# V rows requested over three pairs with the beacon rows last, and sums moved from the tail into the loop

## Chip, cores, metric

The kernel runs on one core of a Trainium2 chip. The metric is the time of one execution on the device in microseconds (us), lower is better. The profile's span, from the first to the last instruction, is some 2 us shorter than that time. Inside the text, moments are us from the start of the span. Executions of this kernel scatter by 1 to 2%, so small differences are read from the profiles' stages as well as from the times.

## The reference

Causal attention with 16 extra "beacon" keys and values per head, then a soft mixture of experts with 32 slots over all 4608 tokens. Cut to what matters:

```python
B, H, S, Nb, D = 8, 8, 576, 16, 64          # attention; E=8 experts, 4 slots each, F=1024
k_all = np.concatenate([beacon_k, k], axis=2)
v_all = np.concatenate([beacon_v, v], axis=2)
scores = q @ k_all^T / 8, causal over k, beacons always visible
x = softmax(scores) @ v_all                 # -> (B*S, H*D) = (4608, 512)
logits = x @ phi                            # (4608, 32)
d = softmax(logits, axis=0);  slot_input = d.T @ x
slot_out[e] = relu(slot_input[e] @ w1[e]) @ w2[e]
c = softmax(logits, axis=1);  out = c @ slot_out
```

## The kernel before

The loop runs over 32 pairs of heads, n = 0 to 31, four pairs to a batch (b = n // 4, g = n % 4). The order of instructions on each engine is the order of the program. Each pair has four score steps on TensorE, an exponential after each on ScalarE, causal masks on GpSimd, the attention matmuls of the pair before, normalisation and copies on VectorE. GpSimd also requests V and the experts' weights, because both are cast from f32 to f16 on the way in. SyncE requests q and k, five pairs ahead.

```python
    def score(n, st):                       # cut: tiles and offsets
        for (c, kn, u0, un, col) in steps[st]:
            for a in range(2):
                nc.tensor.matmul(sc[0:kn, a, col:col + un], kT..., qT..., start=True, stop=True)
        nc.scalar.activation(e, sc[:, :, 0:w], AF.Exp, scale=scale)
        for m, o in diag[st]:
            nc.gpsimd.affine_select(out=e[0:m, :, o:o + m], ...)          # causal mask

    def load_v(b, qd):                      # one quarter of a batch's V rows (cut: batches 0 and 1)
        nc.gpsimd.dma_start(out=vbuf[b % 2][32 * qd:32 * qd + 32, :], in_=...)

    def load_bv(b):                         # beacon rows: inside the first quarter's rows
        nc.gpsimd.dma_start(out=vbuf[b % 2][0:4 * H:4, 0:Nb * D], in_=beacon_v[b]...)

    # ahead of the loop
    for qd in range(4): load_v(0, qd)
    for i in range(3):  load_tail(0, i)
    for qd in range(4): load_v(1, qd)

    for n in range(NP):
        score(n, 0); transp(m, 0); score(n, 1)       # transp: q, k of a later pair, on TensorE
        turn_v(...)                                  # V quarters transposed on VectorE
        attend_head(n - 1, 0); xt_piece(n - 2)
        score(n, 2); transp(m, 1); load_more(m); score(n, 3)
        attend_head(n - 1, 1); normalize(n - 1)
        if n >= 6 and g == 3:      dt_piece(b - 1)
        if n >= 5 and g in (1, 2): logit_piece(b - 1, g - 1)
        if n >= 8 and g == 0:      add_si(si_products(b - 2))
        if n >= 5:
            x, y = divmod(n - 5, 4)
            if x + 3 < B and y < 2:
                load_v(x + 3, 2 * y); load_v(x + 3, 2 * y + 1)
            if y == 1 and x + 3 < B:
                load_bv(x + 3)
        # then some weights (load_w), on a schedule by n
    # tail: last pair, sums of batch 6, last logits, fold_si, dt_piece(L), col_sums(0, 4), si_half,
    # first_layer / turn_hidden / second_layer over four groups of two experts
    # (col_sums(4, 9) in the second group), scaling, output
```

The softmax here doesn't subtract the row's maximum and nothing guards it: scores larger than these inputs give would overflow.

Of the kernel before, what the change touches and what calls it, by code (L numbers as in the profile page):

```python
# [8 lines left out]
FP = mybir.dt.float32  # L9
# [8 lines left out]
def kernel(  # L18
# [13 lines left out]
    P = 128  # L32
# [125 lines left out]
    def turn_tail(b4, hf):  # L158
        turn(vt[b4].bitcast(FP).rearrange("p r e -> p e r")[0:96], vlast[0:96], hf)
# [52 lines left out]
    for qd in range(4):  # L212
        load_v(1, qd)
# [11 lines left out]
    eLh = const.tile([P, Nb + N], F16, name="eLh")  # L225
# [70 lines left out]
    def attend_head(n, a, dst=None):  # L296
        b, g = divmod(n, H // 2)
        dst = av[:, a, :] if dst is None else dst
        for i in range(NCH):
            m = P if i < 4 else UL  # L300
            for c in range(i + 1):
                kn = P if c < 4 else UL
                o, w = blk[(c, i)]
                nc.tensor.matmul(  # L304
                    dst[0:m, i * DD:(i + 1) * DD],
                    ex[n][0:kn, o + a * w:o + a * w + m],
                    vchunk(b, 2 * g + a, c, kn),
                    start=(c == 0), stop=(c == i))
# [48 lines left out]
    def dt_piece(b):  # L357
        dT[b] = sml.tile([P, NCH, NSL], F16, name="dT", tag="dT")
        tp = ps_tr.tile([P, NCH, NSL], F16, name="tr", tag="tr")
        for i in range(NCH):  # L360
            m = P if i < 4 else UL
            nc.tensor.transpose(tp[0:m, i, :], eLh[0:NSL, b * S + P * i:b * S + P * i + m],
                                idh[0:NSL, 0:NSL])
        nc.vector.tensor_copy(out=dT[b][:, 0:4, :], in_=tp[:, 0:4, :])
        nc.vector.tensor_copy(out=dT[b][0:UL, 4, :], in_=tp[0:UL, 4, :])
        nc.vector.memset(dT[b][0:Nb, 0, :], 0.0)
# [26 lines left out]
    def fold_si():  # L393
        tp = ps_tr.tile([P, NDC, NSL], FP, name="tr", tag="tr")
        for c in range(NDC):
            x = siacc[:, 256 * (c // 2):256 * (c // 2) + 256].rearrange("p (f r) -> p f r", r=2)
            nc.tensor.matmul(tp[:, c, :], x[:, :, c % 2], fold[:, :], start=True, stop=True)
        nc.vector.tensor_copy(out=siT[:, :, :], in_=tp[:, :, :])

    def load_more(m):  # L400
        if m + 5 < NP:
            load_pair(m + 5)

# [10 lines left out]
    for n in range(NP):  # L414
# [3 lines left out]
        if 5 <= n and m < NP:  # L418
            transp(m, 0)
        score(n, 1)  # L420
        if n < 5:
            transp(m, 0)
# [4 lines left out]
        if 13 <= n < 17:  # L427
            turn_tail(1, n - 13)
        if 2 <= n < 5:
            attend_head(n - 2, 0)  # L430
        elif n >= 5:
            attend_head(n - 1, 0)
# [6 lines left out]
        if m < NP:  # L439
            transp(m, 1)  # L440
            if n > 0:
                load_more(m)
        score(n, 3)
        if n == 0:
            hold(3)
            load_pair(3)
            nc.sync.dma_start(out=bkf[:, 1:B, :], in_=bks[:, 1:B, :])
            load_pair(4)
            load_more(0)
            load_more(1)  # L450
            nc.sync.dma_start(out=phif[:, :, :], in_=moe_phi.rearrange("(c p) e -> p c e", p=P))
        if n == 1:
            turn_v(0, 2)
            turn_v(0, 3)
            for y in range(4):
                turn_tail(0, y)
# [13 lines left out]
        if n >= 6 and g == 3:  # L470
            dt_piece(b - 1)
# [25 lines left out]
        if n >= 5:  # L497
            x, y = divmod(n - 5, 4)
            if x + 3 < B and y < 2:
                load_v(x + 3, 2 * y)  # L500
                load_v(x + 3, 2 * y + 1)
            if y == 1 and x + 3 < B:
                load_bv(x + 3)
        if 8 <= n < 11:
            load_tail(1, n - 8)
        want = n - 1 if n < 4 else n if n < 6 else 5 + 18 * (n - 5) // 25 if n < 24 else (
            18 + 9 * (n - 23) // 5)
        while wl < min(want, NPC) and not (n < 24 and n % 4 == 2):
            load_w(wl)
            wl += 1  # L510
# [3 lines left out]
    G = 4  # L514
    NG = N // (P * G)
    csp = scs[1][:, 0, :]
    rc = const.tile([P, NG * G], FP, name="rc")

    def etok(cg, j):
        o = Nb + cg * P * G  # L520
        return eLh[:, o:o + P * G].rearrange("p (t j) -> p t j", j=G)[:, :, j]

    def col_sums(c0, c1):
        for i in range(c0 * G, c1 * G):
            nc.tensor.matmul(csp[:, i:i + 1], etok(i // G, i % G)[0:NSL], ones[0:NSL, :],
                             start=True, stop=True)
# [7 lines left out]

    xt_piece(NP - 2)
    avl = [av[:, 0, :], scs[1][:, 1, :]]
    for a in range(2):
        attend_head(NP - 1, a, avl[a])
        normalize_head(NP - 1, a, avl[a])
    sp = si_products(L - 1)  # L540
    lps = [scs[0][:, hf, 0:S // 2] for hf in range(2)]
# [9 lines left out]
    last_logits(range(NDC - 1))  # L551
    xt_piece(NP - 1)
    add_si(sp)
# [4 lines left out]
    fold_si()  # L558
    dt_piece(L)
    col_sums(0, 4)  # L560
# [51 lines left out]
    for p in range(EP + 2):  # L612
# [4 lines left out]
        if p == 1:  # L617
            col_sums(4, NG)
            col_sum_factors()
# [58 lines left out]
```

## Time and profile before

| | before |
|---|---|
| time, median of the first 3 runs | 203.93 us (202.47 to 205.74) |
| span of the profiled run | 201.6 us, mean TensorE clock 0.90 |
| pair 6 starts / pair 31 starts | 39.0 / 150.5 |
| second layer ends / span ends | 173.3 / 201.6 |
| last packet of the loads ends | 169.7 |

The profiled run took 203.51 us.

### The profile page before, as it was taken

What the parts mean: (1) busy time and instruction counts of PE and PEld (TensorE: products, weight loads), DVE (VectorE), ACT (ScalarE), POOL (GpSimd) and SP (SyncE); (2) the same over time, 40 slices, a digit from 0 to 9 for tenths busy, and PEclk for the clock granted to TensorE, in tenths of its full rate; (3) what the DMA queues carried; (4) which work ended last, traced back from release to release, by engine and by line L of the source; (5) the groups of instructions that cost most, each with busy time, mean ns of one, the idle gap of its engine ahead of it and who ended that gap; (6) DMA issues with size and microseconds to landing.
All of it is one profiled execution on the core that took longest, in us unless ns stands there. A gap on an engine that the chain in (4) does not pass through costs nothing.

```text
span 201.6 us, 7189 instructions
## 1 busy us (share of the span) xinstructions
PE 161.2 (80%) x3056; PEld 106.9 (53%) x3056; DVE 137.3 (68%) x286; ACT 129.3 (64%) x189; POOL 110.7 (55%) x285
## 2 busy tenths in 40 slices
PE   6656977895699779969999999999997899788000
PEld 2434756663476547746777766667666654332000
DVE  4446677787188949995989988989855542599100
ACT  2783964786179837964898988898896122399000
POOL 8459689561668586856797577778768000000000
PEclk9975799999589988996999999999999969999855
DMA  6999989999999999999889999999999994099994
GB/s 185 265 267 329 330 217 204 256 252 262 290 265 281 247 203 227 283 265 186 258 174 289 253 294 261 284 222 211 217 214 211 215 211 83 22 400 418 419 423 197
DMA packets 20464, 50.84 MB, mean 252 GB/s; under 512 B 5456, under 2 KB 5456, under 8 KB 19408
## 3 DMA queue, kind: packets, MB, share of 16 engines
q0 software_dynamic: 8048, 21.74, 56.0%
q1 hardware_dynamic: 12240, 28.35, 39.0%
q8 instruction: 24, 0.39, 0.7%
q10 hardware_dynamic: 144, 0.29, 0.5%
q14 instruction: 8, 0.07, 0.1%
HBM read 62.65 MB, written 9.44 MB: 358 GB/s over the span
## 4 chain that ended last, share of the span: by engine, by line
PE 46%; DMA 20%; POOL 10%; DVE 10%; issue 4%; ACT 3%; DVEq 0%; POOLq 0%; ACTq 0%
DMA vbuf<-in_v_dram 20%; PE av L304 14%; PE sc L283 11%; PE tr L266 7%; POOL ex L292 5%; DVE arena L641 4%; PE tr L339 3%; DVE xb L315 2%; ACT ex L290 2%; PE tr L385 2%; PE av L606 2%; PE av L592 1%; PE sc L592 1%; POOL vbuf L162 1%; PE tr L350 1%
## 5 line engine op out<-in xcount | busy, mean ns | idle before, releaser
L290 ACT ACTIVATE ex<-sc 128x736 f16<-128x736 f32 (+1 forms) x124 | 102.0, 868 | 30.2 <-PE sc L283 29.6
L292 POOL TENSOR_SCALAR_AFFINE_SELECT ex<-ex 128x256 f16<-128x256 f16 (+1 forms) x155 | 57.3, 404 | 26.4 <-ACT ex L290 26.1
L304 PE MATMUL av<-vh,ex 128*128 128x65 f16 x854 | 40.6, 202 | 11.6 <-POOL ex L292 9.7
L304 PEld LDWEIGHTS <-ex 128*128 128x128 f16 x930 | 37.3, 109 | 23.7 <-issue 11.9
L283 PE MATMUL sc<-qT,kT 64*128 64x336 bf16 (+5 forms) x384 | 47.4, 300 | 2.9 <-ACT ex L290 1.6
L266 PE MATMUL tr<-idb,arena 64*64 64x64 bf16 x1152 | 32.3, 200 | 3.4 <-DMA arena<-in_k_dram 1.6
L266 PEld LDWEIGHTS <-arena 64*64 64x64 bf16 x1152 | 24.9, 113 | 13.9 <-issue 8.2
L272 DVE COPY qT<-tr 128x576 bf16<-128x576 bf16 x32 | 24.0, 751 | 6.4 <-PE tr L266 5.5
L315 DVE TENSOR_TENSOR xb<-av,r 128x640 f16<-128x640 f32 x31 | 25.6, 825 | 1.1
L283 PEld LDWEIGHTS <-kT 64*128 64x128 bf16 (+1 forms) x384 | 16.4, 100 | 17.1 <-issue 9.5
L272 DVE COPY kT<-tr 128x576 bf16<-128x576 bf16 x27 | 20.4, 755 | 5.9 <-PE tr L266 5.8
L151 DVE STREAM_TRANSPOSE vh<-vbuf 128x256 f32<-128x256 f32 x32 | 20.4, 655 | 2.0 <-DMA vbuf<-in_v_dram 1.4
L343 DVE COPY xT<-tr 128x592 f16<-128x592 f16 x32 | 13.9, 439 | 10.7 <-PE tr L339 10.7
L183 POOL DMA_DIRECT2D arena<-in_moe_w_dram x32 | 17.9, 564 | 0.2
L127 POOL DMA_DIRECT2D vbuf<-in_v_dram x27 | 15.1, 568 | 0.5 <-DVE xb L315 0.5
L339 PE MATMUL tr<-idh,xb 128*128 128x128 f16 (+1 forms) x160 | 14.0, 221 | 0.9 <-DVE xb L315 0.9
L639 ACT ACTIVATE arena<-fp,rc 128x512 f32<-128x512 f32 (+1 forms) x18 | 11.3, 673 | 5.4 <-PE fp L637 4.6
L314 DVE RECIPROCAL r<-av 128x10 f32<-128x10 f32 x31 | 6.9, 221 | 11.2 <-PE av L304 10.9
L641 DVE TENSOR_SCALAR arena<-fp,rc 128x512 f32<-128x512 f32 (+1 forms) x19 | 12.6, 731 | 0.4 <-PE fp L637 0.4
L637 PE MATMUL fp<-soh,eLh 128*128 128x512 f16 (+1 forms) x37 | 10.7, 371 | 2.4 <-ACT arena L639 1.6
L339 PEld LDWEIGHTS <-xb 128*128 128x128 f16 (+1 forms) x160 | 10.3, 102 | 1.2 <-DVE xb L315 1.0
L162 POOL DMA_DIRECT2D vbuf<-in_beacon_v_dram x7 | 3.8, 546 | 11.6 <-DMA vbuf<-in_v_dram 11.6
(98 smaller groups left out, 138.3 us busy)
## 6 DMA issues: line engine op xcount, KB each, us to landing
arena<-in_moe_w_dram POOLq DMA_DIRECT2D x32, 512.0 KB, 10.1
arena<-in_q_dram SPq DMA_DIRECT2D x32, 288.0 KB, 7.5
arena<-in_k_dram SPq DMA_DIRECT2D x31, 288.0 KB, 7.5
out_dram<-arena SPq DMA_DIRECT2D x8, 1024.0 KB, 9.5
vbuf<-in_v_dram POOLq DMA_DIRECT2D x30, 128.0 KB, 6.5
arena<-in_v_dram POOLq DMA_DIRECT2D x4, 128.0 KB, 7.7
out_dram<-arena SPq DMA_DIRECT2D x2, 256.0 KB, 2.7
out_dram<-arena SPq DMA_DIRECT2D x1, 512.0 KB, 3.2
```

Of the source, the lines that this page charges most:

```text
L127: nc.gpsimd.dma_start(out=vbuf[b % 2][32 * qd:32 * qd + 32, :], in_=bass.AP(tensor=v.tensor, offset=v.offset + lo, ap=[hs_, cs_, [1, TK * ...
L151: nc.vector.transpose(out=dst[:, e], in_=src.bitcast(FP).rearrange("p (j e) -> p e j", j=TK)[:, e])
L183: nc.gpsimd.dma_start(out=arena[:, wloc[m]:wloc[m] + WP], in_=src)
L266: nc.tensor.transpose(tp[po:po + 64, j, :], hi, idb[po:po + 64, po:po + 64])
L272: nc.vector.tensor_copy(out=dst, in_=src)
L283: nc.tensor.matmul(sc[0:kn, a, col:col + un], kT[n % 3][64 * a:64 * a + 64, P * c:P * c + kn], qT[n % 3][64 * a:64 * a + 64, u0:u0 + un], ...
L290: nc.scalar.activation(e, sc[:, :, 0:w], AF.Exp, scale=scale)
L292: nc.gpsimd.affine_select(out=e[0:m, :, o:o + m], in_=e[0:m, :, o:o + m], compare_op=AL.is_ge, fill=0.0, base=0, pattern=[[0, 2], [1, m]], ...
L304: nc.tensor.matmul(dst[0:m, i * DD:(i + 1) * DD], ex[n][0:kn, o + a * w:o + a * w + m], vchunk(b, 2 * g + a, c, kn), start=(c == 0), stop= ...
L315: nc.vector.tensor_tensor(out=xb[b % 2][:, :, 2 * g:2 * g + 2, :].rearrange("p i a d -> p a i d"), in0=avv[:, :, :, 0:D], in1=r5[:, :, :]. ...
L339: nc.tensor.transpose(tp[:, i, 0:m], xb[b % 2][0:m, i, 2 * g:2 * g + 2, :].rearrange("p h d -> p (h d)"), idh[0:m, 0:m])
L641: nc.vector.tensor_scalar(out=osb[:, j, c], in0=fp_[:, c], scalar1=rc[:, i:i + 1], scalar2=None, op0=AL.mult)
```

## The change

The intent: take the wait for V off GpSimd, where it holds up the masks; put the first masks ahead of V of batch 1; and shorten the tail. The diff, cut to its core:

```diff
-    for qd in range(4):
-        load_v(1, qd)                      # ahead of the loop
@@ in the loop
+        if n == 0:
+            load_v(1, 0)
         if n == 1:
+            for y in range(1, 4):
+                load_v(1, y)
+        if n == 2:
+            warm(4)                        # dummy matmuls ahead of the first attention
+            if n == 1:
+                warm(2)                    # ahead of transp(m, 1)
-        if n >= 5:
-            x, y = divmod(n - 5, 4)
-            if x + 3 < B and y < 2:
-                load_v(x + 3, 2 * y)
-                load_v(x + 3, 2 * y + 1)
-            if y == 1 and x + 3 < B:
-                load_bv(x + 3)
+        x, y = divmod(n - 4, 4)
+        if n >= 4 and x + 3 < B:
+            for qd in ((0,), (1, 2), (3,), ())[y]:
+                load_v(x + 3, qd)
+            if y == 2:
+                load_bv(x + 3)
-        want = n - 1 if n < 4 else n if n < 6 else 5 + 18 * (n - 5) // 25 if n < 24 else (...)
-        while wl < min(want, NPC) and not (n < 24 and n % 4 == 2):
+        want = n if n < 6 else n - (n - 2) // 4 if n < 24 else 18 + 9 * (n - 23) // 5
+        while wl < min(want, NPC):
@@ sums
+        if n == NP - 1:
+            dt_piece(b - 1)                # between score(n, 0) and score(n, 1)
         score(n, 1)
+        if n == NP - 1:
+            add_si(si_products(b - 1))
+            if n >= 8 and g == 0:
+                col_sums(b - 2, b - 1)     # ahead of attend_head(n - 1, 0)
@@ tail
+    for a in range(2):                     # last token chunk of the last pair first
+        attend_blocks(NP - 1, a, avl[a], [(c, 4) for c in range(NCH)])
     xt_piece(NP - 2)
-    sp = si_products(L - 1)
+    fold_si(0)                             # fold_si in halves, around xt_piece(NP - 1)
     xt_piece(NP - 1)
-    add_si(sp)
+    fold_si(1)
-    fold_si()
+    col_sums(6, 7)
+    for _ in range(3):                     # fillers while ScalarE works
+        nc.tensor.matmul(scs[0][:, 1, :], idh[:, :], xT[L][:, 0, 0:512], start=True, stop=True)
     dt_piece(L)
-    col_sums(0, 4)
...
-            col_sums(4, NG)
+            col_sums(7, NG)
```

More of the change, by code (lines that the diff above doesn't have):

```diff
@@ L224 @@
     xb = [const.tile([P, NCH, H, D], F16, name=f"xb{i}") for i in range(2)]
-    eLh = const.tile([P, Nb + N], F16, name="eLh")
+    eLh = const.tile([P, Nb + N + P - UL], F16, name="eLh")
+    nc.vector.memset(eLh[:, Nb + N:], 0.0)
     nc.vector.memset(eLh[:, 0:Nb], 0.0)
@@ L294, in score, with attend_head, attend_blocks @@
                                     pattern=[[0, 2], [1, m]], channel_multiplier=-1)
-    def attend_head(n, a, dst=None):
+    def attend_head(n, a):
+        attend_blocks(n, a, av[:, a, :], [(c, i) for i in range(NCH) for c in range(i + 1)])
+    def attend_blocks(n, a, dst, blocks):
         b, g = divmod(n, H // 2)
-        dst = av[:, a, :] if dst is None else dst
-        for i in range(NCH):
+        for c, i in blocks:
             m = P if i < 4 else UL
-            for c in range(i + 1):
-                kn = P if c < 4 else UL
-                o, w = blk[(c, i)]
-                nc.tensor.matmul(
-                    dst[0:m, i * DD:(i + 1) * DD],
-                    ex[n][0:kn, o + a * w:o + a * w + m],
-                    vchunk(b, 2 * g + a, c, kn),
-                    start=(c == 0), stop=(c == i))
+            kn = P if c < 4 else UL
+            o, w = blk[(c, i)]
+            nc.tensor.matmul(
+                dst[0:m, i * DD:(i + 1) * DD],
+                ex[n][0:kn, o + a * w:o + a * w + m],
+                vchunk(b, 2 * g + a, c, kn),
+                start=(c == 0), stop=(c == i))
     def normalize(n):
@@ L357, in dt_piece @@
     def dt_piece(b):
-        dT[b] = sml.tile([P, NCH, NSL], F16, name="dT", tag="dT")
+        dT[b] = sml.tile([P, NCH, NSL], F16, name="dT", tag="dT", bufs=2)
         tp = ps_tr.tile([P, NCH, NSL], F16, name="tr", tag="tr")
         for i in range(NCH):
-            m = P if i < 4 else UL
+            m = P if i < 4 or b == B - 1 else UL
             nc.tensor.transpose(tp[0:m, i, :], eLh[0:NSL, b * S + P * i:b * S + P * i + m],
                                 idh[0:NSL, 0:NSL])
-        nc.vector.tensor_copy(out=dT[b][:, 0:4, :], in_=tp[:, 0:4, :])
-        nc.vector.tensor_copy(out=dT[b][0:UL, 4, :], in_=tp[0:UL, 4, :])
+        if b == B - 1:
+            nc.vector.tensor_copy(out=dT[b][:, :, :], in_=tp[:, :, :])
+        else:
+            nc.vector.tensor_copy(out=dT[b][:, 0:4, :], in_=tp[:, 0:4, :])
+            nc.vector.tensor_copy(out=dT[b][0:UL, 4, :], in_=tp[0:UL, 4, :])
         nc.vector.memset(dT[b][0:Nb, 0, :], 0.0)
@@ L391, in add_si, with fold_si @@
         nc.vector.tensor_tensor(out=siacc[:, :], in0=siacc[:, :], in1=sp[:, :], op=AL.add)
-    def fold_si():
-        tp = ps_tr.tile([P, NDC, NSL], FP, name="tr", tag="tr")
-        for c in range(NDC):
-            x = siacc[:, 256 * (c // 2):256 * (c // 2) + 256].rearrange("p (f r) -> p f r", r=2)
-            nc.tensor.matmul(tp[:, c, :], x[:, :, c % 2], fold[:, :], start=True, stop=True)
-        nc.vector.tensor_copy(out=siT[:, :, :], in_=tp[:, :, :])
+    fsp = {}
+    def fold_si(h):
+        if h == 0:
+            fsp[0] = scs[0][:, 1, 0:NDC * NSL].rearrange("p (c s) -> p c s", c=NDC)
+        for c in (2 * h, 2 * h + 1):
+            x = siacc[:, 256 * h:256 * h + 256].rearrange("p (f r) -> p f r", r=2)
+            nc.tensor.matmul(fsp[0][:, c, :], x[:, :, c % 2], fold[:, :], start=True, stop=True)
+        if h == 1:
+            nc.vector.tensor_copy(out=siT[:, :, :], in_=fsp[0])
     def load_more(m):
@@ L402, in load_more, with etok, col_sums @@
             load_pair(m + 5)
+    G = 4
+    NG = N // (P * G)
+    csp = av[:, 0, 400:512]
+    rc = const.tile([P, NG * G], FP, name="rc")
+    def etok(cg, j):
+        o = Nb + cg * P * G
+        return eLh[:, o:o + P * G].rearrange("p (t j) -> p t j", j=G)[:, :, j]
+    def col_sums(c0, c1):
+        for i in range(c0 * G, c1 * G):
+            nc.tensor.matmul(csp[:, i:i + 1], etok(i // G, i % G)[0:NSL], ones[0:NSL, :],
+                             start=True, stop=True)
     for r in range(2):
@@ L469 @@
             load_more(7)
-        if n >= 6 and g == 3:
+        if 6 <= n < NP - 1 and g == 3:
             dt_piece(b - 1)
@@ L505 @@
             load_tail(1, n - 8)
-        want = n - 1 if n < 4 else n if n < 6 else 5 + 18 * (n - 5) // 25 if n < 24 else (
-            18 + 9 * (n - 23) // 5)
-        while wl < min(want, NPC) and not (n < 24 and n % 4 == 2):
+        want = n if n < 6 else n - (n - 2) // 4 if n < 24 else 18 + 9 * (n - 23) // 5
+        while wl < min(want, NPC):
             load_w(wl)
@@ L513 @@
         wl += 1
-    G = 4
-    NG = N // (P * G)
-    csp = scs[1][:, 0, :]
-    rc = const.tile([P, NG * G], FP, name="rc")
-    def etok(cg, j):
-        o = Nb + cg * P * G
-        return eLh[:, o:o + P * G].rearrange("p (t j) -> p t j", j=G)[:, :, j]
-    def col_sums(c0, c1):
-        for i in range(c0 * G, c1 * G):
-            nc.tensor.matmul(csp[:, i:i + 1], etok(i // G, i % G)[0:NSL], ones[0:NSL, :],
-                             start=True, stop=True)
     def col_sum_factors():
@@ L533 @@
     L = B - 1
+    avl = [scs[0][:, 0, :], av[:, 1, :]]
+    for a in range(2):
+        attend_blocks(NP - 1, a, avl[a], [(c, 4) for c in range(NCH)])
     xt_piece(NP - 2)
-    avl = [av[:, 0, :], scs[1][:, 1, :]]
     for a in range(2):
-        attend_head(NP - 1, a, avl[a])
+        attend_blocks(NP - 1, a, avl[a], [(c, i) for i in (3, 2, 1, 0) for c in range(i + 1)])
         normalize_head(NP - 1, a, avl[a])
-    sp = si_products(L - 1)
-    lps = [scs[0][:, hf, 0:S // 2] for hf in range(2)]
+    lps = [scs[1][:, hf, 0:S // 2] for hf in range(2)]
     def last_logits(ts):
```

## The prediction

> **What bounds the kernel now.** Times below are microseconds (us) from the start of the span, and n is the pair of heads (32 pairs, four to a batch). I read the page's costliest groups first.
>
> ```profile
> L292 POOL TENSOR_SCALAR_AFFINE_SELECT ex<-ex 128x256 f16<-128x256 f16 (+1 forms) x155 | 57.3, 404 | 26.4 <-ACT ex L290 26.1
> ...
> L162 POOL DMA_DIRECT2D vbuf<-in_beacon_v_dram x7 | 3.8, 546 | 11.6 <-DMA vbuf<-in_v_dram 11.6
> ```
>
> GpSimd makes the causal masks (L292) and requests V and the weights. Its masks are what the attention matmuls need. L162, the request for a batch's beacon rows, kept it idle for 11.6 us in five waits. It waits because its rows lie inside the part of the V buffer that the batch's own request also writes. The chain of waits (start, length, what) shows this on the path that ends the kernel:
>
> ```profile
> 38.18 11.22 DMA vbuf<-in_v_dram
> 49.68 0.53 POOL vbuf L162
> ...
> 61.63 6.63 DMA vbuf<-in_v_dram
> ...
> 80.87 6.52 DMA vbuf<-in_v_dram
> ```
>
> The 11.22 is a transfer's whole life, not a loss. The loss is in GpSimd's timeline, where the bracket gives the idle time ahead of the row:
>
> ```profile
> 43.52 1.09 POOL L127 DMA_DIRECT2D vbuf<-in_v_dram  x2
> 49.68 0.53 POOL L162 DMA_DIRECT2D vbuf<-in_beacon_v_dram  x1 [5.07 <-DMA vbuf<-in_v_dram]
> 50.21 1.40 POOL L292 TENSOR_SCALAR_AFFINE_SELECT ex<-ex 128x256 f16<-128x256 f16 x4
> ```
>
> The next masks come only at 50.21, and TensorE's first attention matmul after them had waited 4.03 us. The true loss is therefore the lengthening of a pair. From the starts of each pair's first score matmul an undisturbed pair takes 3.9 us. The pair n=8 took 9.9, n=12 took 7.2 and n=16 took 6.9; around n=20 nothing was lost, at n=22 to 23 about 1. Excess: 6.0 + 3.3 + 3.0 + 1 = **13.3 us**, of which the slow clock after the wait is a part (columns: stretch, length, five engines' busy time, TensorE clock, DMA share, GB/s written):
>
> ```profile
> 47.10:57.00 9.90, 5.87 (x94) 3.88 (x93) 4.23 (x11) 3.82 (x5) 5.03 (x15) 0.66 1.07 281
> 57.00:60.90 3.90, 3.90 (x90) 2.79 (x91) 3.71 (x8) 3.16 (x4) 2.51 (x7) 1.00 1.06 253
> 60.90:64.80 3.90, 3.90 (x90) 2.79 (x91) 3.46 (x7) 3.61 (x7) 3.57 (x9) 1.00 1.05 294
> ...
> 131.00:169.00 38.00, 35.31 (x666) 23.63 (x664) 24.68 (x61) 23.88 (x38) 18.92 (x48) 0.96 1.04 210
> ```
>
> The first row is pair 8, at a clock of 0.66; the next two are pairs that run at pace with TensorE busy throughout. The last row is the warning: from 131 on the DMA engines are full (share 1.04) until the last weight is in. The queues say how much they carry:
>
> ```profile
> q0 software_dynamic: 8048, 21.74, 56.0%
> q1 hardware_dynamic: 12240, 28.35, 39.0%
> ...
> HBM read 62.65 MB, written 9.44 MB: 358 GB/s over the span
> ```
>
> q0 casts f32 to f16, so its 21.74 MB written are 43.5 MB read. With q1's 28.35 - 9.44 (output) = 18.9 MB, the loads read 62.4 MB. From the packet records, the last load packet ends at 169.7, so the mean over 167 us is 374 GB/s. Where both queues are always busy, slices of 4 us read 403 to 416 GB/s; with weights alone, 418 to 426. The weights' requests late in the kernel:
>
> ```profile
> L183 POOL DMA_DIRECT2D arena<-in_moe_w_dram x4: 535/540/545, 151.5 to 155.8; - x4
> ...
> DMA to landing us min/median/max: 11.1/12.7/14.2
> ```
>
> The last is issued at 155.8, and a request takes up to 14.2 us, because six earlier ones are still queued ahead of it. Who needs it? The tail on TensorE:
>
> ```profile
> 159.24 1.10 PE L397 MATMUL tr<-fold,siacc 128*128 128x32 f32 x8 [0.28 <-DVE siacc L391]
> ...
> 160.42 0.67 PE L525 MATMUL sc<-ones,eLh 32*128 32x1 f16 x16
> ...
> 171.40 1.91 PE L606 MATMUL av<-arena,hbuf 128*32 128x512 f16 x32
> ```
>
> L606 at 171.40 is the last two groups of the second layer; the second of them reads the last weights at about 172.3. **The last weight thus has only some 2.5 us of slack**, though no wait shows it. After it come 0.9 us of normalisation (L625, to 174.3) and 27.3 us of output, which is 9.44 MB at about 420 GB/s.
>
> **What the Trainium skill says.** (1) "DMA: Bandwidth & Descriptors", section "Two DMAs through the same engine are not ordered": make the issuing engine wait on the first DMA's semaphore before it issues the dependent one. The trace agrees: 5.07 us at L162. (2) The same page, "Where 436 GB/s comes from", gives a fabric ceiling of 435 GB/s and says that loads from HBM are bound at about 358 per core. Here weights alone are read at 418 to 426, so for this single core the first figure is the near one and the second is too low. (3) The same page, "SWDGE vs HWDGE vs iDMA": a cast during a DMA can be issued from GpSimd only. Hence V and weights share q0 and the mask engine, as the trace shows. (4) "TensorE: Matmul & The Clock Gate", Part 1: idleness halves the clock. The trace agrees: 0.50 from 15 to 20, 0.66 in pair 8.
>
> **The change, part by part.**
>
> *Beacon rows last, over three pairs.* Instead of two requests in each of two pairs and the beacon behind them, the first quarter is asked for in n=4k, two in n=4k+1, the last and the beacon in n=4k+2. Only the first quarter overlaps the beacon rows, and it is now asked for two pairs, 7.8 us, earlier; V took 11.1 to 11.6 us to land at pair 7 but 6.5 in the median. The L162 wait should fall from 11.6 to 1 or 2. The number of requests is the same. If compute alone mattered, this is worth 12 of the 13.3 us.
>
> *Batch 1 of V behind the first masks.* Now the first mask of pair 0 runs at 16.0 although its scores' exponentials end at 10.3, because seven requests stand in front of it. In the changed order five masks move ahead of them. TensorE's attention at 17.84 waited 1.62 for them, but it also needs the V transposes, which end at 15.6, and the tail transposes, which end at 17.6. So the wait itself yields about 1. Six dummy matmuls (warm) keep the clock up: two heads at 1.00 instead of 0.61, two transpose groups at 0.62 instead of 0.40, about 1.5. Against that, batch 1 of V is requested about 1.3 later and a weight is put behind it; its transpose at 23.58 may wait 1 to 2. Net for n=6: 1.5 to 2 us earlier (39.0 becomes about 37).
>
> *Column sums and batch 6's sums into the loop.* In the tail 36 column-sum matmuls become 12; the row of 16 cost 0.6 and the row of 20 some 0.7, so 24 fewer are 0.8. The fold's 1.1 us (159.24) no longer stands between the last logits and the exponentials' transposes. The products (0.5) and the addition leave, and the last chunk's blocks of pair 31 no longer wait for its last mask (about 0.7). Three filler matmuls keep the clock, which was 0.74 from 160 to 165, and save part of the first layer's 1.4 + 1.7 against 1.0 each. Sum: 3 to 4 us. The loop takes on 24 tiny matmuls, under 1 us in all, partly in TensorE's idle time.
>
> *Weights' order of request.* The first is asked for in n=1 and not n=3, one a pair until n=5, then three per batch; 18 instead of 17 are out before n=24. These last 14 alone are 14.7 MB, 35 us at 424.
>
> *Sum.* Compute alone: 12 + 1.7 + 3.5 = 17 us off, a time near 187. Now the loads. By 36 us the kernel before had read 11.3 MB. The new one should have as much by then, or some 0.5 MB more thanks to the early weights. Left: 51 MB, at 410 to 415 GB/s = 123 to 124 us, so 159 to 160 with no gap at all. A few gaps of the kind seen at 100 (226 GB/s in a slice) add 1 to 2: **the last load ends at 160 to 162, not 169.7**, 8 to 9.7 us earlier. Four pairs at pace ask for 2.36 MB of q and k, 1.1 of V and 3.15 of weights: 6.6 MB in 15.6 us is 423 GB/s, so the freed loop asks for all that the DMA engines give and cannot stay at 3.9 us a pair. Adding the 2.5 us of slack now used up, the end moves by 10.5 to 12 us. From 203.9: 192 to 193.5. I take **192.5 us**.
>
> **Rivals.** (a) *Compute stays the bound*: all stalls go and the loads keep up, time 186 to 188. For it: the chain before holds no weight at all. Against it: it would need about 62.4 MB by 153, 416 GB/s on average from the start, though the first 36 us had only 11.3 MB. (b) *The waits only move*: in the built program every GpSimd DMA waits for the one issued eight before it. With a full queue of weights, eight of them take 8 x 1.05 MB / 424 = 20 us, while pairs 24 to 31 ask for two a pair, eight in 15.6 us. GpSimd would then stop at L183 rather than L162, and the masks behind it with it, late in the loop: 194 to 197. For it: landing times already rise from 9 to 14 us there. Against it: only the last pairs are hit, and that loss overlaps the wait for the weights. I expect some of this inside my number. (c) *V late*: if the transposes of V wait on VectorE, normalisation does too; 1 us a batch would give 195 or more. Little in the trace is for it beyond batch 1. (d) *Nothing gained*, since DMA was nearly full: over 200 would need the loads to stay at 382 GB/s after 36 us; but the gaps stood in stretches that the stalls left empty, so I give this little.
>
> **Range and chances.** 188 if loads have no gap and the mixed rate reaches 418; 197 if (b) or (c) cost 4 us more. A gain of 2% is any time under 199.9, well above the range: faster 0.95, same 0.04, slower 0.01.
>
> **What would show it.** L162's idle time 2 us or less and no pair over 6 us from n=7 to 22; the first mask near 11; reads of 400 or more in nearly all slices from 40 on; the last load packet at 160 to 162; in the tail a DMA wait on weights ahead of L606's or L592's counterpart, or GpSimd waiting for DMA at L183; output still 27 us after the scaling. I am wrong if the last weight lands well before its reader (then (a)), or if the pairs of the middle loop are all slow at a DMA rate below 390 (then (c) or starved q and k).

## The result and the profile after

The changed kernel took 196.24 us in the median of 4 runs (195.91 to 197.01), the kernel before 204.46 (4 runs, 202.47 to 205.74). The ratio is 0.9635 (95% interval 0.9553 to 0.9717). A ratio is the mean time of one kernel's fast runs over that of the other's of the same rounds, so it is not quite the ratio of the medians. Executions over 1.5% slower than the fastest of the same kernel are left out of the means. The stages:

| us from the start of the span | before | after | difference |
|---|---|---|---|
| pair 6 starts | 39.0 | 39.0 | 0 |
| pair 31 starts | 150.5 | 142.6 | -7.9 |
| pair 6 to pair 31 | 111.5 | 103.6 | -7.9 |
| pair 31 to end of second layer | 22.8 | 23.4 | +0.6 |
| second layer's end to the span's end | 28.3 | 28.6 | +0.3 |
| last packet of the loads | 169.7 | 161.6 | -8.1 |
| reads in the loop, 40 to 130 | 370 GB/s | 403 GB/s | |

The whole gain lies in the loop. GpSimd's list of waits (who waits for whom: us in total, times, longest) answers the line of L162:

```profile
POOL ex L291 <- ACT ex L289: 30.5, 52, 1.9
...
POOL vbuf L162 <- DMA vbuf<-in_v_dram: 2.1, 1, 2.1
```

The beacon wait fell from 11.6 us in five waits to 2.1 in one, at the start (pair 4). What it had cost TensorE shows in TensorE's own list of waits for the loop, before and after:

```profile
PE av L304 <- POOL ex L292: 7.9, 3, 4.0
```

```profile
PE av L304 <- POOL ex L291: 0.2, 1, 0.2
```

Pair 8, which took 9.9 us, and the whole loop from pair 6 to 31 (columns as in the prediction: stretch, length, busy time of TensorE, its weight load, VectorE, ScalarE and GpSimd, clock, DMA share, GB/s written):

```profile
46.60:50.80 4.20, 4.18 (x95) 2.90 (x94) 3.86 (x11) 3.54 (x5) 2.62 (x8) 1.00 1.05 292
39.00:142.60 103.60, 99.47 (x2176) 70.58 (x2175) 89.64 (x175) 86.09 (x126) 77.26 (x204) 1.00 1.06 265
```

The loop of the kernel before in the same view:

```profile
39.00:150.50 111.50, 101.75 (x2152) 71.50 (x2151) 89.58 (x175) 86.64 (x126) 77.78 (x205) 0.94 1.03 247
```

The clock no longer drops (1.00 for 0.94), TensorE is busy 99.5 of 103.6 us, and the DMA share is 1.06 over the loop. (The share sums the times of packets that can overlap, so it passes 1. It hardly tells the two kernels apart, 1.03 and 1.06; the rate of the reads does, 370 and 403 GB/s.) An unstalled pair still takes 3.9 us, as before. But the 25 pairs take 103.6 us and not 25 x 3.9 = 97.5. The weights late in the kernel, and the queues on the page:

```profile
L183 POOL DMA_DIRECT2D arena<-in_moe_w_dram x5: 535/545/545, 139.8 to 149.0; - x5
...
DMA to landing us min/median/max: 10.9/12.3/12.9
```

```profile
q0 software_dynamic: 8048, 21.74, 56.4%
...
q8 instruction: 24, 0.39, 0.7%
...
HBM read 62.65 MB, written 9.44 MB: 371 GB/s over the span
```

The last weight's request goes out at 149.0 and its last packet ends at 161.6, where the prediction had 160 to 162. The q0 traffic is the same number of bytes. The tail on TensorE:

```profile
154.25 1.90 PE L615 MATMUL sc<-arena,siz 128*32 128x512 f16 x16
155.94 1.86 PE L615 MATMUL av<-arena,siz 128*32 128x512 f16 x16
...
164.05 1.91 PE L629 MATMUL av<-arena,hbuf 128*32 128x512 f16 x32
```

L629 at 164.05 is the last two groups of the second layer, so the last group starts near 165.0, 3.4 us after the last load packet (before: 172.3 and 169.7, 2.6 us). The loads did not become the thing that ends the tail.

### The profile page after: what moved, and what is told of

Read it like the earlier page. It is cut to its first block, busy times and chain, and to the rows that moved or that the text cites. A ratio compares the mean times of both kernels' runs of the same rounds, so it can differ in the third digit from the quotient of the medians.

```text
span 194.5 us, 7202 instructions
## 1 busy us (share of the span) xinstructions
PE 162.3 (83%) x3065; PEld 106.3 (55%) x3065; DVE 137.6 (71%) x286; ACT 128.5 (66%) x189; POOL 111.0 (57%) x285
## 3 DMA queue, kind: packets, MB, share of 16 engines
HBM read 62.65 MB, written 9.44 MB: 371 GB/s over the span
## 4 chain that ended last, share of the span: by engine, by line
PE 50%; DVE 12%; DMA 10%; ACT 10%; POOL 6%; issue 4%; DVEq 1%
PE av L304 13%; PE sc L282 11%; PE tr L265 8%; ACT ex L289 6%; DMA arena<-in_v_dram 5%; DMA vbuf<-in_beacon_v_dram 5%; DVE arena L664 4%; PE tr L339 3%; PE sc L239 3%; DVE xb L315 3%; POOL ex L291 2%; PE av L629 2%; ACT kT L269 2%; PE tr L350 2%; PE sc L615 1%
## 5 line engine op out<-in xcount | busy, mean ns | idle before, releaser
L289 ACT ACTIVATE ex<-sc 128x736 f16<-128x736 f32 (+1 forms) x124 | 101.4, 869 | 23.0 <-PE sc L282 22.5
L282 PE MATMUL sc<-qT,kT 64*128 64x336 bf16 (+5 forms) x384 | 46.6, 295 | 3.4 <-ACT ex L289 1.4
L304 PEld LDWEIGHTS <-ex 128*128 128x128 f16 (+1 forms) x930 | 36.1, 106 | 16.9 <-issue 15.7
L304 PE MATMUL av<-vh,ex 128*128 128x65 f16 (+1 forms) x854 | 39.8, 198 | 4.8 <-DVE xb L315 2.3
L265 PE MATMUL tr<-idb,arena 64*64 64x64 bf16 x1152 | 31.6, 199 | 1.0 <-DVE xT L343 0.7
L265 PEld LDWEIGHTS <-arena 64*64 64x64 bf16 x1152 | 24.4, 112 | 11.4 <-issue 8.5
L183 POOL DMA_DIRECT2D arena<-in_moe_w_dram x32 | 18.0, 564 | 0.2
L662 ACT ACTIVATE arena<-fp,rc 128x512 f32<-128x512 f32 (+1 forms) x18 | 11.3, 673 | 5.4 <-PE fp L660 4.6
L314 DVE RECIPROCAL r<-av 128x10 f32<-128x10 f32 x31 | 6.8, 219 | 10.7 <-PE av L304 10.3
L339 PE MATMUL tr<-idh,xb 128*128 128x128 f16 (+1 forms) x160 | 13.7, 215 | 0.2 <-issue 0.2
L339 PEld LDWEIGHTS <-xb 128*128 128x128 f16 (+1 forms) x160 | 9.8, 99 | 0.5 <-issue 0.3
L350 PE MATMUL tr<-xT,phih 128*128 128x288 f16 x56 | 9.2, 285 | 0.8 <-ACT kT L269 0.7
```

The lines of the kernel that those rows point to most:

```text
L183: nc.gpsimd.dma_start(out=arena[:, wloc[m]:wloc[m] + WP], in_=src)
L265: nc.tensor.transpose(tp[po:po + 64, j, :], hi, idb[po:po + 64, po:po + 64])
L282: nc.tensor.matmul(sc[0:kn, a, col:col + un], kT[n % 3][64 * a:64 * a + 64, P * c:P * c + kn], qT[n % 3][64 * a:64 * a + 64, u0:u0 + un], ...
L304: nc.tensor.matmul(dst[0:m, i * DD:(i + 1) * DD], ex[n][0:kn, o + a * w:o + a * w + m], vchunk(b, 2 * g + a, c, kn), start=(c == 0), stop= ...
L339: nc.tensor.transpose(tp[:, i, 0:m], xb[b % 2][0:m, i, 2 * g:2 * g + 2, :].rearrange("p h d -> p (h d)"), idh[0:m, 0:m])
```

## The experiments

Twelve runs were made, one of them (x11) of the changed kernel again. Every one was timed in rounds with the kernel before on the same chip; medians and ratios are to those runs.

| run | edit | this | before | ratio (interval) | pair 6 to 31 | pair 31 to second layer's end |
|---|---|---|---|---|---|---|
| x1_b_vorder | before + V order alone | 196.06 | 202.83 | 0.9679 (0.9643-0.9716) | 104.1 | 21.2 |
| x2_a_oldv | change - V order | 201.62 | 202.83 | 0.9867 (0.9806-0.9927) | 108.4 | 21.7 |
| x3_a_halfw | change, half the weights | 189.47 | 202.83 | 0.9342 (0.9276-0.9407) | 98.2 | 21.7 |
| x4_a_nowarm4 | change - four dummy matmuls | 195.69 | 202.83 | 0.9629 (0.9572-0.9686) | 104.2 | 21.7 |
| x9_b_tail | before + tail part alone | 203.42 | 202.98 | 0.9995 (0.992-1.0071) | 109.5 | 21.7 |
| x5_a_dtlate | change, batch 6's sums later | 195.18 | 202.98 | 0.9613 (0.954-0.9686) | 104.7 | 20.9 |
| x6_a_colsumtail | change, column sums in the tail | 195.51 | 202.98 | 0.9632 (0.9587-0.9677) | 103.7 | 21.9 |
| x7_a_fill | change + five fillers | 195.83 | 202.98 | 0.9644 (0.959-0.9698) | 103.3 | 22.1 |
| x10_b_prologue | before + prologue part alone | 203.37 | 204.21 | 1.014 (0.9988-1.0291) | 113.4 | 22.8 |
| x8_combo | x4 and x5 together | 196.33 | 204.21 | 0.9756 (0.9626-0.9886) | 104.4 | 20.9 |
| x11_after | the changed kernel again | 195.91 | 204.21 | 0.9785 (0.9655-0.9914) | 103.7 | 21.7 |
| x12_a_fewinstr | change, 400 TensorE instructions fewer | 195.89 | 202.59 | 0.9651 (0.9547-0.9755) | 104.7 | 21.7 |

In the third call (x10, x8, x11) one of the eleven runs of before took 199.30 us and made nine others count as slow, so that these three ratios rest on two runs of before; they came out "unclear" and I compare x8 and x11 with each other. The medians in the table hold slow runs too; the ratios do not.

### Which part gave the gain

x1 put the new V order alone into the kernel before:

```diff
-        if n >= 5:
-            x, y = divmod(n - 5, 4)
-            ... two quarters in each of two pairs, load_bv at once behind them
+        x, y = divmod(n - 4, 4)
+        if n >= 4 and x + 3 < B:
+            for qd in ((0,), (1, 2), (3,), ())[y]:
+                load_v(x + 3, qd)
+            if y == 2:
+                load_bv(x + 3)
```

> The kernel before with one part of the change alone: a batch's V rows over three pairs and the beacon rows last (weights' schedule, prologue and tail as before). Theory 1, from the two traces: nearly all of the gain is the beacon wait, and TensorE then sets the loop's pace. L162's idle time falls from 11.6 us to under 3, no pair of the middle over 5.5 us, and the time is 195 to 197, as the whole change or a little better, since the loop carries no column sums. Theory 2, from my prediction: the loads set the pace; with the old weights' order the last load ends some 2 us later than with the whole change and the time is 198 to 200.

It took 196.06 us, 0.9679, nearly the whole of the change's 0.9635. L162's idle time fell to 0.9 us, and the longest pair from 7 to 22 took 5.1:

```profile
POOL vbuf L162 <- DMA vbuf<-in_v_dram: 0.9, 1, 0.9
```

So the V order is nearly the whole gain, as the first theory said (its other half, that TensorE then sets the pace, is taken up with x3 and x12). With the old weights' schedule the last load did end later, at 163.2 against 161.6, but this did not cost the 2 us of the second theory.

x2 did the reverse, undoing the V order in the changed kernel (the same lines the other way round).

> The changed kernel with its V order undone (two rows requests in each of two pairs, beacon behind them at once), all else as changed. If the V order is the whole gain: the beacon waits are back at 10 us or more, time 203 to 205, like before. If the other parts (masks ahead of batch 1, column sums and sums of batch 6 moved, weights earlier) carry a gain of their own as I predicted (5 us): 198 to 200.

Its median is 201.62 us (199.28 to 203.73), but two of its four runs count as slow. The two fast ones average 199.9, which is in the range I gave for parts with a gain of their own, and the ratio of 0.9867 rests on them. The beacon waits are back:

```profile
POOL vbuf L162 <- DMA vbuf<-in_v_dram: 8.5, 5, 2.6
```

That is less than the 10 us I expected and than the 11.6 and 5.1 of before. So 1.3% remains without the V order.

x9 gave the kernel before the tail part alone, and x10 the prologue part alone:

```diff
+ x9:  column sums in the loop, batch 6's sums in pair 31, fold in halves, last blocks first, 3 fillers
+ x10: load_v(1, 0) at n == 0, load_v(1, 1..3) at n == 1, warm(2), warm(4)
```

> The kernel before with the third part alone: column sums into the loop, sums of batch 6 into pair 31, fold in halves, last blocks first, three fillers (V order, prologue and weights as before). My prediction gave this 3 to 4 us: 200 against 203.5. From the two traces, where pair 31's start to the end of the second layer took 22.8 us before and 23.4 after, and each batch of the loop took 0.28 us more of TensorE for the column sums: no gain, 203 to 205, with pair 31 at about the same moment or 1 us later than before.

> The kernel before with the second part alone: batch 1 of V behind the first masks, and the six dummy matmuls. My prediction gave it 1.5 to 2 us. From the traces of the changed kernel and of x4_a_nowarm4, where V of batch 1 is what pair 3 waits for once TensorE is early: nothing, 202.5 to 203.5, n=6 still at 39 to 40; what it gains at the first masks goes into the dummy matmuls or the wait for batch 1.

x9: 0.9995, no gain, and pair 31 at 149.7 against 150.5. x10: unclear. Its fast runs average 203.5, and before's two 200.7, so no gain shows; its pair 6 was at 37.8, a little early, but pair 31 at 151.2. The 1.3% of x2 may then come from the weights' order, from the parts together, or from the beacon waits themselves, which are not the same in every run with the old V order (8.5, 9.5, 11.3 and 11.6 us). I didn't run the weights' order alone, so this stays open.

### Why the prologue gave nothing

In the changed kernel the masks of pair 0 came from 8.05 on, sooner than the predicted 11: the prediction took the end of the last of the four exponentials (10.3), and the first mask needs only the first of them. GpSimd's timeline (start, length, what; in brackets the idle time before):

```profile
8.05 1.03 POOL L291 TENSOR_SCALAR_AFFINE_SELECT ex<-ex 128x256 f16<-128x256 f16 x3 [0.70 <-ACT ex L289]
```

TensorE did not use it. Its timeline in the changed kernel:

```profile
16.29 1.87 PE L239 MATMUL sc<-siacc 128*128 128x512 bf16 x4 [0.21 <-ACT arena L289]
17.95 1.02 PE L304 MATMUL av<-vh,ex 128*128 128x65 f16 x14
```

The four dummy matmuls ran at half clock, one every 0.43 us, and held TensorE until the first attention at 17.95; before, it had started at 17.84. x4 takes them away:

```diff
-        if n == 2:
-            warm(4)
```

> The changed kernel without the four dummy matmuls in pair 2. Theory 1: they hold TensorE for 1.7 us at half clock just when pair 0's masks and V are ready, so the first attention starts near 16.4 instead of 17.95 and n=6 comes 0.8 to 1.5 us earlier than 39.0; time 194.7 to 195.5. Rival: without them the clock comes back later and pairs 2 and 3 lose what was gained: no change, 196 to 196.5. Theory 2 would absorb any gain in the loop, 196 as well, but then n=6 would still be early.

Now the first attention starts at 16.33 and pair 3 at 19.8 instead of 21.4, but pair 6 at 39.8, no earlier than 39.0. TensorE's timeline and then VectorE's:

```profile
16.33 0.63 PE L304 MATMUL av<-vh,ex 128*128 128x65 f16 x14
```

```profile
24.38 0.66 DVE L151 STREAM_TRANSPOSE vh<-vbuf 128x256 f32<-128x256 f32 x1 [2.18 <-DMA vbuf<-in_v_dram]
```

VectorE waits 2.18 us for V of batch 1, which the change requests later. The beacon keys' copies stand behind that transpose, and pair 4's scores behind those. So my own counter-term of 1 to 2 us was right. It took most of the gain: of the 1.6 us that TensorE was ahead of the changed kernel, 0.3 were left at the last attention of pair 4 (31.56 against 31.83). A half-clock stretch from 31.5 to 34.9, which the changed kernel's profile doesn't have, then turned the lead into 0.7 us of delay. The four dummy matmuls thus cost little because the V wait would have taken most of their time anyway.

### Why the tail gave nothing

The first layer's first two groups took 1.90 and 1.86 us in the changed kernel's profile (L615 in the fence above), at half clock:

```profile
154.20:156.00 1.80, 1.75 (x20) 0.74 (x24) 1.44 (x7) 0.00 (x0) 0.00 (x0) 0.50 1.05 212
```

x11 ran the same kernel again, and x7 added five fillers:

```diff
+    filler(3)          # as in the change
     dt_piece(L)
+    filler(3)
...
     si_half(L, ...)
+    filler(2)
```

> The changed kernel once more, beside x8_combo on the same chip. Loop from pair 6 to 31 again 103 to 105 us, with 5 to 8 us of pauses at every 256th instruction; the tail from pair 31 to the end of the second layer 21.7 us if its half-clock stretch does not fall into the first layer, 23.4 if it does.

> The changed kernel with five more filler matmuls in the tail: three behind the last transposes, two behind the last sums. Theory: the first layer's first two groups ran at half clock in the changed kernel's profile (1.90 and 1.86 us against 1.05), because TensorE was idle in bits between 152 and 154; with the fillers they run at full clock, the tail shrinks by 1 to 1.6 us. Rival: the drop comes from the small shapes of the tail, not from the idle bits, or moves with the phase of the clock's window: no change beyond the fillers' own 0.5.

In x11 the same two rows took 1.05 and 1.04 us, without any edit:

```profile
154.78 1.05 PE L615 MATMUL sc<-arena,siz 128*32 128x512 f16 x16
155.65 1.04 PE L615 MATMUL av<-arena,siz 128*32 128x512 f16 x16
```

The half-clock stretch in the tail lasts 3.41 us in each of the three profiles that have one, and in x11 there was none. Of the eleven profiles with the changed tail or nearly so (the result's own and ten experiments, all but x1 and x10), ten show about 1.05 us in both rows. With the old tail it is two of three that have the stretch (before and x10, both 22.8 us; x1 has none). It costs 1.6 to 1.7 us. One kernel can have it or not (the result's profile and x11), but whether the three fillers of the change make it rarer isn't shown: no run takes them out. x7's five more did nothing, 22.1 us against 21.7 for x11. Like is compared with like, then: with the stretch the old tail took 22.8 and the changed one 23.4, without it 21.2 (x1) and 21.7 (x2, x3, x4, x9, x11, x12). Either way the changed tail is longer by about 0.5 us.

Where did the 3 to 4 us go? Cut the tail at two moments, the start of the last transposes of x (the L339 row below) and the last logits' exponentials on ScalarE. TensorE's timeline of x1, then of x11:

```profile
151.01 0.42 PE L339 MATMUL tr<-idh,xb 128*128 128x128 f16 x5
...
152.68 1.10 PE L397 MATMUL tr<-fold,siacc 128*128 128x32 f32 x8 [0.28 <-DVE siacc L391]
...
155.23 1.05 PE L591 MATMUL sc<-arena,siz 128*32 128x512 f16 x16
```

```profile
150.95 0.43 PE L339 MATMUL tr<-idh,xb 128*128 128x128 f16 x5
...
154.00 0.67 PE L376 MATMUL tr<-dT,xb 128*128 128x32 f16 x20 [0.47 <-DVE dT L369]
```

ScalarE starts these exponentials at 152.43 in x1 and at 152.38 in x11, 1.4 us after the transposes in both. From there to the first layer x1 took 2.80 us and x11 2.40 (to 154.78). So the fold and the column sums, counted at 1.9 us in the prediction, gave 0.4: in the old tail most of their time ran while ScalarE and VectorE made what TensorE needed next, and in the changed one fillers and waits stand in their place. Ahead of the transposes the changed tail lost: they start 6.86 us after pair 31 in x1 and 7.81 in x11, 0.95 later. The sum, 0.95 - 0.40 and under 0.1 in the first layer, is the 0.5. The loss ahead of the transposes is what x5 is about, which moves batch 6's sums out of TensorE's way:

```diff
-        if n == NP - 1:
-            dt_piece(b - 1)                # between score(n, 0) and score(n, 1)
         score(n, 1)
-        if n == NP - 1:
-            add_si(si_products(b - 1))
...
         score(n, 2)
+        if n == NP - 1:
+            dt_piece(b - 1)
...
+    add_si(si_products(L - 1))             # after the loop
```

> The changed kernel with the sums of batch 6 later: their transposes after pair 31's third score step, their products and the addition after the loop. Theory: in the changed kernel these stand in TensorE's order ahead of the third score step, wait 0.7 us for ScalarE and VectorE and take 1 us, so that the exponentials (idle 1.25 us there) and the last masks come 1.2 us later. Later placement gives that back: pair 31's start to its last mask falls from 5.8 to about 4.7 us, the time falls by 0.8 to 1.2 us. Rival: what the products take after the loop comes back as tail time, no change within 0.4.

ScalarE's exponentials of pair 31, x11 first and then x5:

```profile
143.91 1.45 ACT L289 ACTIVATE ex<-sc 128x736 f16<-128x736 f32 x2
146.59 1.86 ACT L289 ACTIVATE ex<-sc 128x928 f16<-128x928 f32 x2 [1.24 <-PE sc L282]
```

```profile
144.92 3.40 ACT L289 ACTIVATE ex<-sc 128x736 f16<-128x736 f32 x4
```

With the sums inside pair 31 ScalarE waits 1.24 us for the third score step; with the sums later, the four exponentials run in one piece, and the transposes start 7.01 us after pair 31. The tail fell from 21.7 to 20.9 us in the profile, 0.8 as expected. In the time it is within the scatter (0.9613 against 0.9635, intervals overlapping).

x6 put the column sums back into the tail:

```diff
-            if n >= 8 and g == 0:
-                col_sums(b - 2, b - 1)
...
-    col_sums(6, 7)
...
     dt_piece(L)
+    col_sums(0, 4)
...
-            col_sums(7, NG)
+            col_sums(4, NG)
```

> The changed kernel with all column sums back in the tail (16 after the last transposes, 20 in the first layer, as before). Theory: in the loop they cost TensorE 0.28 us a batch (1.7 us in all) and 48 more instructions to fetch, and in the tail 24 of them cost 0.8; the time falls by about 1 us. Prediction: the loop's cost hides in idle TensorE, the time rises by 0.8.

Neither: 0.9632, the same. The tail took 21.9, and the loop took 103.7 although 1.7 us of TensorE's work had left it. This was a sign that something other than TensorE's work sets the loop's pace.

### What sets the pace of the loop

The 103.6 us exceed the loop's bare pace, the 98.1 us that x3 shows below, by some 5.5. Through the loop neither TensorE nor VectorE shows a wait for data of more than 0.8 us in all. What TensorE shows are pauses "issue", for which the profile has no releaser:

```profile
PE av L304 <- issue: 2.1, 5, 0.8
PE sc L282 <- issue: 0.6, 2, 0.3
PE tr L265 <- issue: 0.4, 1, 0.4
```

One of them, in TensorE's timeline:

```profile
118.44 0.33 PE L304 MATMUL av<-vh,ex 128*128 128x65 f16 x5
119.61 0.46 PE L304 MATMUL av<-vh,ex 128*128 128x65 f16 x9 [0.85 <-issue]
```

I numbered TensorE's instructions in the trace's records and took, for each, the time from its predecessor's start less the median of that kind of step. Of the excesses above 0.12 us that recur, all fall on the same place: instruction 188 of every 256. There are twelve in the loop, 0.14 to 1.01 us, 5.5 us together, whatever the instruction is. The page's queue q8 ("instruction", above) moves 24 packets of 16,384 bytes: one block of 256 instructions of 64 bytes each, and 24 such blocks are 6144 instructions, where the trace has 6130 of TensorE. In the loop such a packet starts every 6.08 us (standard deviation 0.16), and the first instruction of the block starts 2.2 to 2.8 us later (the last block, used in the tail, 5.3), never sooner. So TensorE waits there for its own instructions, whose packets the page counts among those of the same 16 DMA engines as the data. "Runtime: NRT & Kernel Launch", section "Instruction fetch mechanics", of the Trainium skill describes blocks of 16 KiB (256 instructions) through a DMA queue of the sequencer's own; the trace agrees with both. It says that the cost of crossing a block is mostly hidden; here 5.5 us are not.

x3 asks whether the data traffic makes the blocks late:

```diff
     def load_w(i):
         e, r = divmod(m, 4)
+        if e % 2:
+            return                         # odd experts not loaded; readers use the even ones
```

> The changed kernel, wrong on purpose: only the even experts' weights are loaded (16 requests and 16.8 MB of reads less), the odd experts' matmuls read the even ones' copies. Theory 2 (loads set the pace): the loop falls to its bare matmul pace and the end moves by 6 us or more, to 188 to 190. Theory 1 (TensorE sets the pace; the extra over the bare pace is a pause at every 256th TensorE instruction, where the next block of instructions is fetched by DMA behind the data): the pauses shrink from 5.5 us in the loop to 1 to 3, the rest stays; 191 to 194. If the pauses do not depend on the data traffic: no change, 195 to 196.5.

The result was wrong, as intended. The pauses fell from 5.5 to 0.7 us and the loop to its bare pace:

```profile
40.30:138.40 98.10, 97.26 (x2176) 69.91 (x2175) 88.48 (x175) 85.70 (x126) 69.92 (x190) 1.00 0.88 216
```

The DMA share is 0.88 here, TensorE is busy 97.3 of 98.1 us, and the time was 189.47: the range of theory 2 (188 to 190), and pauses below the 1 to 3 us of theory 1. (x3 also takes requests off GpSimd, but in the changed kernel's loop TensorE waited for GpSimd's masks only 0.2 us.) So x3 shows that the traffic is the cause, but not in which form. Either each block takes a fixed 6.1 us under load, or the loads as a whole are the pace, and late blocks are where it surfaces. x12 separates them. It keeps the data and most of the work, and drops 9% of the loop's TensorE instructions:

```diff
+        if i == 1 and n >= 7:              # second head of k: one matmul in place of nine transposes
+            nc.tensor.matmul(tp[64:128, :, :]...bitcast(FP), idb[64:128, 64:128], idb..., start=True, stop=True)
         for j in range(J):
-            for po in (0, 64):
+            for po in (0, 64)[:1 if i == 1 and n >= 7 else 2]:
```

> The changed kernel, wrong on purpose: from pair 7 on the nine transposes of K's second head are one matmul with 288 columns, so 400 TensorE instructions of 4349 fall out of the loop (9%), while the same data is loaded and TensorE's bare work falls by little (0.20 to about 0.15 us a pair, 1 us in all). In all variants with full loads the loop from pair 6 to 31 took 103.3 to 104.7 us and an instruction block of 256 came every 6.1 us. Theory A, a fixed time per block under load: 15.4 blocks at 6.1 us are 94, so the bare work binds and the loop takes 97 to 98, time 189 to 190. Theory B, the rate of all loads together is the pace (40.4 MB at 404 GB/s in 100 us) and late instruction blocks are only where it shows: the loop stays at 102 to 104, blocks come every 6.6 us or data waits appear in their place, time 195 to 196.5.

The loop took 104.7 us, a little over the 102 to 104 of theory B and far from the 97 to 98 of theory A, and the time was 195.89: theory B. (The result passed the comparison all the same; that says only that the output hardly depends on which keys the second head attends to.) The block pauses fell to 0.2 us, and blocks now come every 6.5 us. In their place TensorE and VectorE wait for data in the loop:

```profile
PE tr L270 <- DMA arena<-in_k_dram: 2.5, 3, 1.1
...
PE tr L270 <- DMA arena<-in_q_dram: 1.1, 1, 1.1
```

```profile
DVE vh L151 <- DMA vbuf<-in_v_dram: 2.2, 2, 1.6
```

In the changed kernel these rows were absent or below 0.9. With 9% fewer instructions the same loss shows as waits for k, q and V. The reads from 40 to 130 were 404 GB/s in x12 and 403 in the changed kernel. A pair asks for 6.6 MB / 4 = 1.65 MB, which at 403 GB/s takes 4.1 us, and 25 pairs 102 us. That is all but 1.6 us of the loop. Why the mixed reads stop at 403 and not at the 420 or so of weights alone, no run here shows.

### An attempt to beat it

x8 joined x4 and x5:

> The changed kernel without the four dummy matmuls and with the sums of batch 6 later (x4 and x5 together), an attempt to beat it. If the tail's 0.8 us of x5 is real it stays, since the tail is not in the stretch where instruction blocks arrive late: ratio to before 0.958 to 0.961 against 0.962 to 0.964 for the changed kernel on the same chip. If the differences were those of the clock's phase: no difference.

Its profile kept the 20.9 us of tail, but its fast runs average 195.85 us against 196.11 for x11 on the same chip: no difference that these runs can show. No version here beats the changed kernel clearly.

## Why the prediction was right, and where it was not

The time, 196.24, lies inside the range of 188 to 197, though 3.7 us above the 192.5 that I took, and 2% faster was nearly certain. That the range held is partly luck: I kept its upper end for rivals (b) and (c), which did not come, and the tail and the prologue filled that room. By its steps:

- **The beacon wait goes.** Right: 11.6 to 2.1 us, no pair from 7 to 22 over 4.8, and x1 shows that this part is nearly the whole gain.
- **The freed loop asks for all that DMA gives and cannot stay at 3.9 us a pair.** Right in mechanism. The loop takes 103 to 105 us in every variant with the new V order and full loads, whether TensorE's work is made smaller (x1, x6) or its instructions fewer (x12), and 98.2 with half the weights (x3). I had expected this to show as late V or as GpSimd waiting at L183. It showed as late instruction blocks, which I had not thought of; rivals (b) and (c) did not occur in the changed kernel.
- **The last load at 160 to 162.** Right: 161.6.
- **"Adding the 2.5 us of slack now used up."** This is the step that failed. The slack between the last packet and its reader was 3.4 us and not 0. The loads' end moved by 8.1 us and the span's end by 7.1, as the tail is longer by 0.6 and the output by 0.3; 10.5 to 12 were expected. The prediction called itself wrong if the last weight landed well before its reader, and read that as rival (a), compute as the bound. The sign came, but (a) does not hold: the loads pace the loop (x3, x12), and TensorE's work in the tail then stands between the loop and that reader.
- **The tail, 3 to 4 us off.** Wrong: +0.6 between two profiles that both have a half-clock stretch there, +0.5 between profiles without it. The term was mis-sized twice. I counted the bare time of what left the tail, but between the last logits and the first layer only 0.4 us of it was on the path, since TensorE waited there for ScalarE and VectorE. And I gave nothing for what pair 31 took on: there the sums stand ahead of a score step in TensorE's order and delay the last exponentials by 1.2 us, of which x5 gets 0.8 back. This is also why the slack stayed: the tail did not get short enough to run into the weights.
- **The prologue, 1.5 to 2 us.** Wrong: 0 (pair 6 at 39.0 in both). The parts given there, about 1 and 1.5 less 1 to 2, make 0.5 to 1.5 and not 1.5 to 2. The dummy matmuls run at half clock in front of the work that they are to speed up, and without them V of batch 1 is late (x4). It may have changed little in the end: the changed kernel reads 403 to 410 GB/s from 20 to 32 us already. No run tests this.
- **A slip without consequence.** The 27.3 us after the normalisation are not 9.44 MB at 420 GB/s, which would be 22.5: the output's packets run from 176.1 to 200.2, a mean of 391, and the rest lies before and after them.

## What to carry to other kernels

Remove a wait, then ask what the freed engine will ask for: here 6.6 MB a batch at some 404 GB/s set the next bound, and no tuning of TensorE's work in the loop changed the time after that. With the DMA engines full, the shortage showed here as late instruction blocks (5.5 us) and, with fewer instructions, as late k, q and V (x12); a pause without a releaser that recurs every 256 instructions was the sign of it, and taking bytes away was the test. And an item moved out of a tail must be charged where it lands, where it stands in front of what follows in its engine's order; and it gives back only what was on the path there, 0.4 of 1.9 us here.

## What the Trainium skill lacked or had wrong

- "Runtime: NRT & Kernel Launch", "Instruction fetch mechanics": calls the cost of crossing a 16 KiB block mostly hidden. With the DMA share at 1.06, TensorE paused at twelve block boundaries of the loop for 0.14 to 1.01 us, 5.5 us of 103.6; at a share of 0.88 (x3) only 0.7 remained. The page doesn't say that data traffic delays the blocks. When within the preceding block the request is made is not in these records and stays open.
- "DMA: Bandwidth & Descriptors", "Where 436 GB/s comes from": about 358 GB/s per core, half of a stack's, as what binds loads from HBM. With one core at work, weights alone were read at 417 to 427 GB/s in the changed kernel, mixed with q, k and V at about 403. The 425 that the page measured with one core is the figure that fits.
- "TensorE: Matmul & The Clock Gate", Part 1: nothing wrong. The half-clock stretches in the tail are 3.41 us long, the window that it gives, and the dummy matmuls of 512 columns started 0.43 us apart at half clock, as it states. What is lacking is a warning that dummy matmuls issued while the clock is down delay the work behind them: the first attention began at 17.95 with four of them and at 16.33 without (x4).
